# Moving tiles of one-pass float32 products: from starts on a multiple of 64 bytes to starts 8, 16, 24 and 48 bytes past one

## The chip, the core and the metric

The kernel runs on one core of a Trainium2 chip. The metric is the time of one execution on the device in microseconds (us), the median of several runs. A profile of one execution gives the details. Its engines are PE (TensorE, matrix products), PEld (TensorE's weight loads), DVE (VectorE), ACT (ScalarE), POOL (GpSimd) and SP (SyncE, here a queue of transfers).

A matrix product on TensorE has a stationary operand (`lhsT`, 128 x 128, loaded first as weights) and a moving operand (`rhs`, 128 partitions by up to 512 columns) that is read column by column from the on-chip memory SBUF. The change is about where in a partition of SBUF the moving operands begin.

## The reference, cut to what matters

```
attention, for each batch b and head h (8 x 8, 576 tokens, 64 per head):
    q_s = softmax of q over the 64 elements of a token
    k_s = softmax of k over the 576 tokens
    x   = q_s @ (k_s.T @ v)
x becomes 4608 tokens x 512
gated layer (512 -> 1536 -> 512):
    out = (sigmoid(x @ w_gate) * (x @ w_val)) @ w_out
```

All inputs are float32; the weights of the layer arrive as 64-bit words and are narrowed to float32 on the chip.

## The kernel before

**Tiling.** The 4608 tokens are done in 9 passes `w` of 512. A pass holds x transposed (512 features on 4 x 128 partitions, 512 tokens in the row) and runs over the 1536 hidden features in 6 steps of 256. Pass 0 is special: its products are plain float32 (`g1_0`, L610, and `g2_0`, L637), while the weights arrive and are narrowed and split beside it.

**Passes 1 to 8.** For these each float32 number is split into a high part of type float32r and the rest, low; a product takes three products of parts (high x high, high x low, low x high). Products of float32r pass the array once. The first layer (`g1`, L655) saves products by a scheme of Strassen's kind: the 2 x 2 blocks of x give seven combinations (B11, T1, T2, B21, T3, B22, T4), those of the weights seven (A11, S1, S2, A12, S3, S4, A22). A step of `g1` is 7 x 2 x 2 x 3 = 84 products with 256 columns. Stationary are the weights: `a_w` for A11, A12 and A22, `s_sb` for the sums S1 to S4. Moving are the split combinations of x, `c_hl`. They lie in four buffers with the tags c0 (B11, T1), c1 (T2, B21), c2 (T3, B22) and c3 (T4). The second layer (`g2`, L723) is 24 products with 512 columns a step: stationary the gated hidden values `h`, moving the split output weights `wo_hl`, two tiles a step, the first from the tag wo_hl, the second from the tag wo_t.

**What else lies in these buffers.** In pass 0 the c buffers hold raw weights on arrival (`w_raw` in c0 and c1, `wo_raw` in c3) and x of the pass (`x_0` in c2); wo_t and wo_hl hold the output weights while they are narrowed and split. The sums S1 to S4 and the split output weights go out to DRAM once and come back in each step: `s_load` (L278) for the next step after each product that used the sum, and `wo_load` (L234), both on POOL's queue.

**Order.** The order on each engine is written out by hand: in a step come the 84 products of `g1` with their evacuations (L673 to L696 on ACT and DVE), `h_split` (L705, L706), then a piece of the next pass's attention (`side_a`), `g2` of the step before, `wo_load`, and another piece (`side_b`). An engine does its instructions in this order and stops at the first that has to wait. The attention of the next pass runs through a chain of transfers on SP's queue: k_in and qn_in arrive (L331, L432), the rows' largest values go out and come back spread (`qn_send`, `q_spread`), qT_in arrives (L485) and is lessened by them on DVE (`qT_sub`, L489).

**Places in SBUF.** Tiles of a pool stand one behind the other, in order of the pools. The pads `pad_a` (48 floats, 192 bytes) and `pad_w` (80 floats, 320 bytes) shift what follows. Before the change, all c buffers, all wo_t and wo_hl buffers and the `ring` buffers begin 448 bytes past a multiple of 512; `s_sb`, `a_w` and `h` begin 128 bytes past one. All of these are multiples of 64 bytes, and the slices that the products read begin at multiples of 256 bytes within them.

Of the kernel before, what the change touches and what calls it, by code (L numbers as in the profile page):

```python
# [8 lines left out]
F32 = mybir.dt.float32  # L9
F32R = mybir.dt.float32r  # L10
I32 = mybir.dt.int32
# [6 lines left out]
P = 128  # L18
B, H, S, D = 8, 8, 576, 64
DM, DF = 512, 1536  # L20
NTOK = B * S
T = 512
HT = T // 2
NW = NTOK // T
NT = T // P
NP = H // 2
# [25 lines left out]
def attn_moe(ctx: ExitStack, tc: tile.TileContext, qf, qn, qT, k, kT, v, wg, wv, wo, out):  # L52
# [5 lines left out]
    cpool = ctx.enter_context(tc.tile_pool(name="cpool", bufs=1))  # L58
    apad = ctx.enter_context(tc.tile_pool(name="apad", bufs=1))
    apool = ctx.enter_context(tc.tile_pool(name="apool", bufs=1))  # L60
    two = ctx.enter_context(tc.tile_pool(name="two", bufs=2))
    wpad = ctx.enter_context(tc.tile_pool(name="wpad", bufs=1))
    wpool = ctx.enter_context(tc.tile_pool(name="wpool", bufs=2))
    four = ctx.enter_context(tc.tile_pool(name="four", bufs=4))
    ring = ctx.enter_context(tc.tile_pool(name="ring", bufs=11))
    small = ctx.enter_context(tc.tile_pool(name="small", bufs=2))
    apad.tile([P, 48], F32, name="pad_a")
    wpad.tile([P, 80], F32, name="pad_w")
    dpool = ctx.enter_context(tc.tile_pool(name="dpool", bufs=2, space=bass.MemoryType.DRAM))
    spool = ctx.enter_context(tc.tile_pool(name="spool", bufs=1, space=bass.MemoryType.DRAM))  # L70
    ps_acc = ctx.enter_context(tc.tile_pool(name="ps_acc", bufs=NT, space=bass.MemoryType.PSUM))
    ps_gv = ctx.enter_context(tc.tile_pool(name="ps_gv", bufs=3, space=bass.MemoryType.PSUM))
    ps_at = ctx.enter_context(tc.tile_pool(name="ps_at", bufs=1, space=bass.MemoryType.PSUM))

    s_sb = const.tile([P, 4, 2, 2, 2 * P], F32R, name="s_sb")
    x_32 = const.tile([P, NP, T], F32, name="x_32")
# [30 lines left out]
    w_raw = {}  # L107
    wo_raw = {}
    f_w = {}
    a_w = {}  # L110
    wo_t = {}

    def raw_tile(j):

        i = (0, 1, 2, 3, 0, 1, 2, 3, 0, 1, 2, 0)[j]
        if i == 2:
            return sg.rearrange("p q n t -> p (q n t)").bitcast(I32)
        if i == 3:
            return x_32.rearrange("p h t -> p (h t)").bitcast(I32)
        return cpool.tile([P, 4 * DM], I32, name="w_raw", tag=f"c{i}")  # L120

    def load_w(j):
        w_raw[j] = t = raw_tile(j).rearrange("p (n e) -> p n e", n=2)
        for n, src in enumerate((wg, wv)):
            nc.sync.dma_start(out=t[:, n], in_=src[j].bitcast(I32))

    def load_wo(j):
        if j % 3 == 0:
            wo_raw[j] = t = cpool.tile([P, 2 * DM], I32, name="wo_raw", tag="c3")
        else:  # L130
            wo_raw[j] = t = two.tile([P, 2 * DM], I32, name="wo_raw", tag="h_hi")
        nc.sync.dma_start(out=t, in_=wo[j * P:(j + 1) * P].bitcast(I32))
# [11 lines left out]
    def narrow_sign(raw):  # L144

        half = raw.bitcast(F16).rearrange("p (e f) -> p e f", f=4)
        nc.scalar.activation(
            half[:, :, 1], words(raw)[:, :, 1].bitcast(F32), AF.Copy, scale=2.0 ** -100
        )
# [8 lines left out]
    def narrow_abs(raw, w):  # L158
        src = words(raw)[:, :, 1].bitcast(F32)
        if len(w.shape) == 3:  # L160
            src = src.rearrange("p (a b) -> p a b", a=w.shape[1])
        nc.scalar.activation(w, src, AF.Abs, scale=2.0 ** -112)
# [33 lines left out]
    def wo_on_vector(j):  # L196
        return j % 2 and j > 6
# [5 lines left out]

    def wo_top(j):
        if j % 2 == 0:
            wo_t[j // 2] = wpool.tile([P, 2, DM], F32, name="wo_t")
        if not wo_on_vector(j):
            narrow_sign(wo_raw[j])
        narrow_abs(wo_raw[j], wo_t[j // 2][:, j % 2])
# [4 lines left out]
    wo_out = {}  # L214

    def wo_hi(j):
        wo_out[j] = t = wpool.tile([P, 2, DM], F32R, name="wo_hl")
        nc.scalar.copy(out=t[:, 0], in_=wo_t[j // 2][:, j % 2])

    def wo_save(j):  # L220
# [6 lines left out]
    wo_hl = {}  # L227

    def wo_load(w, p):
        wo_hl[w, p] = [  # L230
            wpool.tile([P, 2, DM], F32R, name="wo_hl", tag=tag) for tag in ("wo_hl", "wo_t")
        ]
        for i, t in enumerate(wo_hl[w, p]):
            nc.gpsimd.dma_start(  # L234
                out=t.rearrange("p h e -> p (h e)"), in_=wo_dram[2 * p + i].bitcast(F32R)
            )
# [308 lines left out]
        copy(out=x_32[:, hp], in_=x_ps.pop((w, hp)))  # L545


    x_0 = cpool.tile([P, NP, T], F32, name="x_0", tag="c2")
    q_0 = [two.tile([P, 2, T], F32, name="q_0", tag="h_lo") for _ in range(2)]

    def qT_copy(hp):
# [18 lines left out]
    def quarter(kh, th):  # L570
        return x_32[:, 2 * kh:2 * kh + 2, th * HT:(th + 1) * HT]

    c_32 = {}
    c_hl = {}
# [11 lines left out]

    def c_split(i):
        if i % 2 == 0:
            t = cpool.tile([P, 2 if i < 6 else 1, 2, 2, HT], F32R, name="c_hl", tag=f"c{i // 2}")
            for x in range(i, min(i + 2, 7)):  # L590
                c_hl[x] = t[:, x % 2]
        src = c_32.pop(i) if i in c_32 else quarter(*{B11: (0, 0), B21: (1, 0), B22: (1, 1)}[i])
        hi, lo = (c_hl[i][:, x] for x in range(2))
        nc.scalar.copy(out=hi, in_=src)
        nc.vector.tensor_tensor(out=lo, in0=src, in1=hi.bitcast(F32), op=ALU.subtract)
# [115 lines left out]
    def step(w, i):  # L711
        return (i - 1) % NS if w == 1 else i
# [114 lines left out]
    def after_first(j):  # L827
# [34 lines left out]
        if j == 10:  # L862
            c_subs()
            load_next(1, 5, range(2))
            for i in (B11, T1, T2, B21):
                c_split(i)
# [33 lines left out]
    for t in range(5):  # L900
        v_load(0, t, v0[:, t])
    load_wo(0)
    load_w(1)
    load_wo(1)
    load_w(2)
    for g in range(2):
        rows = kT[1, 2 * g * P:2 * (g + 1) * P].rearrange("(g p) s -> p g s", p=P)
        nc.sync.dma_start(out=k1T[:, 2 * g:2 * g + 2], in_=rows)
        for hp in (2 * g, 2 * g + 1):
            kT_load(1, hp, k1T[:, hp])  # L910
    load_w(3)
    load_wo(2)
    for c in range(NC):
        qn_load(1, c)
# [16 lines left out]
    for t in range(2, 5):  # L931
        n = KTILES[t][1]
# [65 lines left out]
    w_top(1)  # L998
    wo_low(0)
    wo_top(0)  # L1000
    w_low(2)
    wo_low(1)
# [3 lines left out]
    for j in range(NJ):  # L1006
# [5 lines left out]
        if j > 0:  # L1012
            wo_hi(j - 1)
        if j + 2 < NJ:
            w_top(j + 2)
        if j + 1 < NJ:
            w_join(j + 1)
            wo_top(j + 1)
# [24 lines left out]
        after_first(j)  # L1043

    wo_hi(NJ - 1)
    g_mul_0(NJ - 1)
    for i in (T3, B22, T4):
        c_split(i)
    wo_save(NJ - 1)

    def wo_next(w, at):
        wo_load(w, step(w, at))

    prev = None
    for w in range(1, NW):
        last = w == NW - 1
        for at in range(NS):
            p = step(w, at)
            end = last and at == NS - 1
            g1(w, p, None if end else step(w + (at + 1) // NS, (at + 1) % NS))  # L1060
            if at == NS - 1 and not last:
                for i in range(7):
                    c_split(i)
            h_split(w, p)
            if not last:
                side_a(w + 1, at)
            if prev is None:
                g2_0(NJ - 1)
                wo_next(1, 0)
                wo_next(1, 1)  # L1070
            else:
                g2(*prev)
                if not end:
                    wo_next(w + (at + 1) // NS, (at + 1) % NS)
            prev = (w, at)
            if not last:
                side_b(w + 1, at)
# [39 lines left out]
```

## Time and profile before

| | us |
|---|---|
| Median of three runs (980.42, 981.57, 981.74) | 981.57 |
| Span of the profiled execution (no other time of it is listed) | 984.2 |
| TensorE busy in it | 954.0 |
| VectorE busy | 613.1 |
| ScalarE busy | 471.4 |
| L655 (`g1`), busy, 4032 products | 483.1 |
| L723 (`g2`), busy, 1152 products | 272.3 |

The span runs from the first to the last instruction of the profiled execution. Rows of groups read: line, engine, operation, output<-input, shape, xcount | busy us, mean ns of one | idle us just before. Rows of stages read: stretch, its length, busy time and count for each engine, then the share of TensorE's clock that was granted, the busy share of the DMA engines, and GB/s. Rows of the timeline read: start, length, engine, line, operation, xcount, and in brackets the idle time before with what ended it. Products overlap: the next starts while the last columns of the one before drain, so the distance of two starts is shorter than the duration of one.

### The profile page before, as it was taken

The page shows a single profiled execution, that of the slowest core. Times are in us where ns is not written, and L with a number is a line of the kernel's source. Part 1 is how long each engine was busy: PE and PEld are TensorE (multiplying, and loading weights), DVE is VectorE, ACT ScalarE, POOL GpSimd, SP SyncE. Part 2 cuts the span into 40 slices and gives each one's busy share as a digit, 9 for nine tenths or more (in the row PEclk, how much of TensorE's full clock was granted, in tenths as well). Part 3 has the DMA queues.
Part 4 walks back from the last instruction along what each step waited for, and adds up shares of the span by engine and source line. Part 5 has one row for each costly group of instructions (what it writes and reads, how often), then busy time and mean ns, then how long its engine had stood idle before and what let it go on. Part 6 is the DMA issues. An engine that isn't in the chain of part 4 may idle for free.

```text
span 984.2 us, 15634 instructions
## 1 busy us (share of the span) xinstructions
PE 954.0 (97%) x6062; PEld 824.0 (84%) x6062; DVE 613.1 (62%) x1013; ACT 471.4 (48%) x812; POOL 167.3 (17%) x316
## 2 busy tenths in 40 slices
PE   5899999799999999999999999999999999999998
PEld 5544544599999999999989999899999999999997
DVE  8688778776666566755684667557654655463242
ACT  4589785553436354525362545353434434533222
POOL 0110001221122112111111111121112121212210
PEclk7899999899999999999999999999999999999999
DMA  9987484899699978998899869996998779858662
GB/s 337 330 244 267 165 291 166 302 350 323 203 245 361 306 229 212 374 284 259 180 381 304 261 143 375 332 276 132 374 317 239 216 237 312 248 176 251 199 206 74
DMA packets 93864, 257.78 MB, mean 262 GB/s; under 512 B 15264, under 2 KB 17568, under 8 KB 93024
## 3 DMA queue, kind: packets, MB, share of 16 engines
q0 software_dynamic: 43712, 168.32, 56.9%
q1 hardware_dynamic: 50080, 88.48, 30.6%
q8 instruction: 48, 0.79, 0.4%
q14 instruction: 24, 0.20, 0.1%
HBM read 228.20 MB, written 28.56 MB: 261 GB/s over the span
## 4 chain that ended last, share of the span: by engine, by line
PE 66%; DMA 17%; DVE 7%; ACT 7%; issue 2%; SPq 1%; POOL 0%; DVEq 0%; ACTq 0%; POOLq 0%
PE gv L655 37%; PE acc L723 19%; DMA ring<-k_in 3%; DMA q_m_row<-q_m 3%; PE gv L610 3%; DMA q_b<-q_m_row 3%; DMA kmax_row<-k_max 2%; PE gv L538 2%; DMA ring<-qT_in 1%; PE at L378 1%; PE acc L637 1%; DMA ring<-qn_in 1%; DMA s<-s_sb 1%; DMA wo<-wo_hl 1%; PE at L538 1%
## 5 line engine op out<-in xcount | busy, mean ns | idle before, releaser
L655 PE MATMUL gv<-c_hl,s_sb 128*128 128x256 f32 x2304 | 288.1, 280 | 4.3 <-ACT sg L673 4.2
L655 PEld LDWEIGHTS gv<-c_hl,s_sb 128*128 128x128 f32 x2304 | 276.7, 188 | 6.9 <-ACT sg L673 6.5
L723 PE MATMUL acc<-wo_hl,h 128*128 128x512 f32 x1152 | 272.2, 392 | 0.0
L723 PEld LDWEIGHTS acc<-wo_hl,h 128*128 128x128 f32 x1152 | 213.1, 188 | 44.3
L655 PE MATMUL gv<-c_hl,a_w 128*128 128x256 f32 x1728 | 226.1, 279 | 0.7 <-DVE a_w L269 0.7
L655 PEld LDWEIGHTS gv<-c_hl,a_w 128*128 128x128 f32 x1728 | 214.9, 188 | 5.2 <-issue 1.0
L278 POOL DMA_DIRECT2D s_sb<-s x188 | 100.1, 532 | 321.8 <-PE gv L655 317.5
L681 DVE TENSOR_TENSOR sg<-gv,sg 128x512 f32<-128x512 f32 x48 | 33.2, 691 | 163.0 <-PE gv L655 163.0
L234 POOL DMA_DIRECT2D wo_hl<-wo x96 | 50.9, 531 | 297.6 <-PE acc L723 295.4
L683 ACT COPY sg<-gv 128x512 f32<-128x512 f32 x48 | 28.1, 586 | 106.4 <-PE gv L655 106.4
L610 PE MATMUL gv<-x,f_w 128*128 128x512 f32 x160 | 72.4, 606 | 5.5 <-ACT h L618 5.5
L673 ACT COPY sg<-gv 128x512 f32<-128x512 f32 x48 | 28.0, 583 | 89.8 <-PE gv L655 65.1
L685 DVE TENSOR_TENSOR sg<-sg 128x512 f32<-128x512 f32 x48 | 33.2, 692 | 58.9 <-ACT sg L683 58.9
L610 PEld LDWEIGHTS gv<-x,f_w 128*128 128x128 f32 x160 | 30.5, 194 | 43.7 <-issue 36.0
L706 DVE TENSOR_TENSOR h<-sg,h 128x1024 fp32r<-128x1024 f32 x48 | 58.8, 1226 | 1.6
L688 ACT ACTIVATE sg<-sg 128x512 f32<-128x512 f32 x48 | 30.3, 632 | 55.8 <-DVE sg L687 55.8
L694 DVE TENSOR_TENSOR sg<-sg 128x512 f32<-128x512 f32 x48 | 33.2, 693 | 33.5 <-ACT sg L688 33.5
L637 PE MATMUL acc<-wo_t,h 128*128 128x512 f32 x96 | 45.3, 617 | 5.7 <-DVE h L622 5.6
L678 ACT COPY sg<-gv 128x512 f32<-128x512 f32 x48 | 28.1, 586 | 44.7 <-PE gv L655 44.7
L637 PEld LDWEIGHTS acc<-wo_t,h 128*128 128x128 f32 x96 | 18.8, 199 | 30.0 <-issue 21.7
L675 ACT COPY sg<-gv 128x512 f32<-128x512 f32 x48 | 28.1, 586 | 26.2 <-PE gv L655 26.1
L412 ACT CAST kv_sb<-kmax_b 64x256 fp32r<-64x256 f32 x14 | 5.7, 404 | 67.1 <-DVE kmax_b L388 66.8
(152 smaller groups left out, 1054.8 us busy)
## 6 DMA issues: line engine op xcount, KB each, us to landing
s_sb<-s POOLq DMA_DIRECT2D x188, 512.0 KB, 7.6
wo_hl<-wo POOLq DMA_DIRECT2D x96, 512.0 KB, 6.0
s<-s_sb POOLq DMA_DIRECT2D x6, 2048.0 KB, 7.6
out<-x SPq DMA_DIRECT2D x36, 256.0 KB, 9.6
ring<-k_in SPq DMA_DIRECT2D x28, 256.0 KB, 15.0
ring<-qn_in SPq DMA_DIRECT2D x28, 256.0 KB, 10.3
q_b<-q_m_row SPq DMA_DIRECT2D x56, 128.0 KB, 8.6
ring<-qT_in SPq DMA_DIRECT2D x28, 256.0 KB, 8.9
```

Of the source, the lines that this page charges most:

```text
L234: nc.gpsimd.dma_start(out=t.rearrange("p h e -> p (h e)"), in_=wo_dram[2 * p + i].bitcast(F32R))
L278: nc.gpsimd.dma_start(out=s_sb[:, i].rearrange("p h n e -> p (h n e)"), in_=s_dram[p][:, i * n:(i + 1) * n].bitcast(F32R),)
L538: nc.tensor.matmul(ps[:, f:t], lhsT=kl if lh else kh, rhs=rh[:, f:t], start=(lh == 0 and rh is qh), stop=(lh == 1),)
L610: nc.tensor.matmul(ps[n], lhsT=w[:, kt // 2, sl], rhs=x_0[:, kt], start=(kt == 0), stop=(kt == NK - 1),)
L637: nc.tensor.matmul(acc[0][m], lhsT=h_0[j][:, m * P:(m + 1) * P], rhs=wo_t[j // 2][:, j % 2], start=(j == 0), stop=(j == NJ - 1),)
L655: nc.tensor.matmul(ps[:, n], lhsT=lh(kt), rhs=c_hl[i][:, x, kt], start=(first and n == 0 and kt == 0 and lh is wh and x == 0), stop=(last ...
L681: nc.vector.tensor_tensor(out=sg[:, 0], in0=rr, in1=sg[:, 0], op=ALU.add)
L685: nc.vector.tensor_tensor(out=sg[:, 3], in0=sg[:, 3], in1=sg[:, 2], op=ALU.add)
L688: nc.scalar.activation(sg[:, 0:2, 0], sg[:, 0:2, 0], AF.Sigmoid)
L694: tt(out=sg[:, 0:2, 0], in0=sg[:, 0:2, 0], in1=sg[:, 0:2, 1], op=ALU.mult)
L706: nc.vector.tensor_tensor(out=lo, in0=sg[:, :, 0], in1=hi.bitcast(F32), op=ALU.subtract)
L723: nc.tensor.matmul(acc[w][m], lhsT=h[lh][:, i, sl], rhs=o[i][:, rh], start=(at == 0 and i == 0 and lh == 0 and rh == 0), stop=(at == NS - ...
```

## The change

The tiles that serve as moving operands get 16 floats more, and what is used of them starts 4, 12, 2, 6, 4 or 12 floats (16, 48, 8, 24, 16 or 48 bytes) behind the start of the buffer, by tag. The pads change with it, so that `a_w`, `h`, `four`, `ring` and all behind them stay where they were modulo 512 bytes. The c buffers, each 64 bytes longer, no longer stand at the same place modulo 512: with the shift, c2 begins 456, c0 16, c3 88 and c1 176 bytes past a multiple of 512. The wo_t buffers come to stand 240 and 304, the wo_hl buffers 336 and 400 past one (worked out from the order and the sizes of the pools). No instruction is added, removed or moved, and no number computed changes.

```
-    apad.tile([P, 48], F32, name="pad_a")
-    wpad.tile([P, 80], F32, name="pad_w")
+    apad.tile([P, 112], F32, name="pad_a")
+    wpad.tile([P, 16], F32, name="pad_w")
...
+    SHIFT = {"c0": 4, "c1": 12, "c2": 2, "c3": 6, "wo_hl": 4, "wo_t": 12}
+
+    def shifted(pool, n, dtype, name, tag):
+        k = SHIFT[tag]
+        return pool.tile([P, n + 16], dtype, name=name, tag=tag)[:, k:k + n]
...
-        return cpool.tile([P, 4 * DM], I32, name="w_raw", tag=f"c{i}")
+        return shifted(cpool, 4 * DM, I32, "w_raw", f"c{i}")
...
-            wo_raw[j] = t = cpool.tile([P, 2 * DM], I32, name="wo_raw", tag="c3")
+            wo_raw[j] = t = shifted(cpool, 2 * DM, I32, "wo_raw", "c3")
...
-            wo_t[j // 2] = wpool.tile([P, 2, DM], F32, name="wo_t")
+            wo_t[j // 2] = shifted(wpool, 2 * DM, F32, "wo_t", "wo_t").rearrange(
+                "p (h e) -> p h e", h=2
+            )
...
-        wo_out[j] = t = wpool.tile([P, 2, DM], F32R, name="wo_hl")
+        wo_out[j] = t = shifted(wpool, 2 * DM, F32R, "wo_hl", "wo_hl").rearrange(
+            "p (h e) -> p h e", h=2
+        )
...
-            wpool.tile([P, 2, DM], F32R, name="wo_hl", tag=tag) for tag in ("wo_hl", "wo_t")
+            shifted(wpool, 2 * DM, F32R, "wo_hl", tag).rearrange("p (h e) -> p h e", h=2)
+            for tag in ("wo_hl", "wo_t")
...
-    x_0 = cpool.tile([P, NP, T], F32, name="x_0", tag="c2")
+    x_0 = shifted(cpool, NP * T, F32, "x_0", "c2").rearrange("p (h t) -> p h t", h=NP)
...
-            t = cpool.tile([P, 2 if i < 6 else 1, 2, 2, HT], F32R, name="c_hl", tag=f"c{i // 2}")
+            n = 2 if i < 6 else 1
+            t = shifted(cpool, n * 4 * HT, F32R, "c_hl", f"c{i // 2}").rearrange(
+                "p (n h k t) -> p n h k t", n=n, h=2, k=2
+            )
```

## The prediction, made before the change was run

> **What bounds the kernel now.** I read the page's busy shares first, then the shares of the chain that ended last, then the busy time by stage, first of all instructions and then of the two lines whose moving tiles change.
>
> ```profile
> PE 954.0 (97%) x6062; PEld 824.0 (84%) x6062; DVE 613.1 (62%) x1013; ACT 471.4 (48%) x812; POOL 167.3 (17%) x316
> ...
> PE 66%; DMA 17%; DVE 7%; ACT 7%; issue 2%; SPq 1%; POOL 0%; DVEq 0%; ACTq 0%; POOLq 0%
> PE gv L655 37%; PE acc L723 19%; DMA ring<-k_in 3%; DMA q_m_row<-q_m 3%; PE gv L610 3%; DMA q_b<-q_m_row 3%; DMA kmax_row<-k_max 2%; PE gv L538 2%; DMA ring<-qT_in 1%; PE at L378 1%; PE acc L637 1%; DMA ring<-qn_in 1%; DMA s<-s_sb 1%; DMA wo<-wo_hl 1%; PE at L538 1%
> ```
>
> ```profile
> 182.00:484.00 302.00, 299.71 (x2130) 279.01 (x2129) 197.04 (x329) 140.66 (x262) 60.26 (x113) 1.00 0.98 277
> 484.00:787.00 303.00, 300.24 (x2130) 280.11 (x2129) 186.95 (x309) 137.06 (x254) 56.82 (x108) 1.00 0.97 280
> 787.00:984.00 197.00, 193.54 (x1334) 179.67 (x1332) 89.43 (x138) 66.11 (x121) 35.51 (x67) 1.00 0.72 213
> ```
>
> ```profile
> 181.60:984.00 802.40, 483.07 (x4032) 478.01 (x4032) 1.00 0.91 262
> ```
>
> ```profile
> 181.60:984.00 802.40, 272.25 (x1152) 213.10 (x1152) 1.00 0.91 262
> ```
>
> From 182 us on TensorE is busy all but 9 of 802 us (302 + 303 + 197 less 299.7 + 300.2 + 193.5), at the full granted clock (1.00 in the third column from the right). The last two rows are L655 alone (4032 products with 256 columns, moving tiles c_hl) and L723 alone (1152 products with 512 columns, moving tiles wo_hl): 483 and 272 us. Each of these products reads a tile that the change moves, so the start-to-start time of a product, which I call its pitch, decides. The timeline of TensorE gives it, since each row shows the start of a run of products and their count.
>
> ```profile
> 350.06 2.88 PE L655 MATMUL gv<-c_hl,s_sb 128*128 128x256 f32 x24
> 352.78 1.52 PE L655 MATMUL gv<-c_hl,a_w 128*128 128x256 f32 x12
> 354.14 2.88 PE L655 MATMUL gv<-c_hl,s_sb 128*128 128x256 f32 x24
> ...
> 358.22 5.66 PE L723 MATMUL acc<-wo_hl,h 128*128 128x512 f32 x24
> 363.72 2.50 PE L538 MATMUL gv<-ring,kv_sb 128*128 128x192 f32 x18
> ```
>
> ```profile
> 945.49 2.99 PE L655 MATMUL gv<-c_hl,s_sb 128*128 128x256 f32 x24
> 948.32 1.58 PE L655 MATMUL gv<-c_hl,a_w 128*128 128x256 f32 x12
> 949.73 2.99 PE L655 MATMUL gv<-c_hl,s_sb 128*128 128x256 f32 x24
> ...
> 953.97 5.67 PE L723 MATMUL acc<-wo_hl,h 128*128 128x512 f32 x24
> 959.48 1.58 PE L655 MATMUL gv<-c_hl,a_w 128*128 128x256 f32 x12
> ```
>
> The same instructions on the same tiles run in **two rhythms**. At 350 us 24 products take 2.72 us (352.78 - 350.06), 113.3 ns each; at 945 us they take 2.83 us, 117.9 ns each. A pass of 24 at L723 takes 5.50 us at 358 us and 5.51 us at 954 us: 229 ns each in both. Within a stretch the pitch is steady. The chain of waits, in order of time, shows whole stretches of 84 products (columns: start, us, what):
>
> ```profile
> 348.87 9.52 PE gv L655 x84
> ...
> 504.80 10.81 DMA q_m_row<-q_m
> 518.04 8.57 DMA q_b<-q_m_row
> 526.68 7.91 DMA ring<-qT_in
> ...
> 944.24 9.89 PE gv L655 x84
> 959.64 9.89 PE gv L655 x84
> ```
>
> Among the pieces that this view lists, 26 are whole stretches of 84; 5 of them take 9.52 us and 21 take 9.89 to 10.10. So four in five have the long pitch. As the rhythm changes between stretches and holds within them, it looks like a matter of how the reading falls against the lines of the memory, which a start address can touch.
>
> What would a product cost with no such loss? Products in plain float32 give a bound, because they read the same tiles and pass the array twice:
>
> ```profile
> 83.85 3.60 PE L637 MATMUL acc<-wo_t,h 128*128 128x512 f32 x8
> 87.28 3.17 PE L610 MATMUL gv<-x,f_w 128*128 128x512 f32 x7
> ```
>
> ```profile
> 625.38 1.95 PE L378 MATMUL at<-v,ring 128*128 128x128 f32 x16
> 627.16 3.04 PE L378 MATMUL at<-f_last,ring 128*128 128x128 f32 x24
> ```
>
> Eight of 512 columns take 3.43 us, 429 ns each, or 214 ns for each of two passes (that there are two is inferred from the time): 15 ns less than the 229 of L723. Sixteen of 128 columns, 256 column passes, take 1.78 us, 111 ns each, and each has a weight load, as each of L655 has. I take 111 ns and 214 ns as the floors of L655 and L723.
>
> The Trainium skill ("TensorE: Matmul & The Clock Gate", Back-to-back issue gap) gives N/2.4 + 2.5 ns for a single warm product, 109 and 216 ns here; the rows above stand 4 to 9 and 13 ns over it. If that held after the change, the sum below would come out at the second rival.
>
> **The change part by part.**
>
> *L655.* Nothing is added or removed: the same 4032 products, from tiles that start 8, 16, 24 or 48 bytes past a line. No row of before has a one-pass product that starts off a multiple of 64 bytes. The nearest is L365, whose moving tile has rows of 129 floats, so its starts walk 4 bytes at a time:
>
> ```profile
> L365 PE MATMUL acc<-lent x13: 269/274/422, 30.1 to 31.8; 128*128 128x129 f32 x9, 64*128 64x129 f32 x4
> ```
>
> ```profile
> L378 PE MATMUL at<-v,ring 128*128 128x128 f32 x112 | 13.6, 275 | 0.0
> ```
>
> Their median of 274 ns is the mean of the aligned L378 products, 275. So at half the reading rate a shifted start costs nothing; at the full rate it is open. Ends: all products at the floor, or one more 64-byte line for each product. A line is 16 columns, 117.9 / 16 = 7.4 ns. I take the value between, **the short pitch in all stretches**, since 113.3 ns is the pitch that the same products already reach and the rhythm depends on where the reading starts. By count 48 x 21/26 = 39 stretches gain 0.37 us (9.89 - 9.52): 14.3 us of TensorE time.
>
> *L723.* The pitch is 229 ns beside either pitch of L655, so I take no change; the ends are -15 ns (the floor) and +7.4 ns (a line) on 1152 products, -17 to +8.5 us.
>
> *What of a gain stays.* Not all of the loop is bound by TensorE. In the chain above the transfers of the attention side follow each other from 504.80 to 534.59 us (526.68 + 7.91), and VectorE waits for the last:
>
> ```profile
> 532.62 2.69 DVE L489 TENSOR_TENSOR ring<-ring,q_b 128x512 f32<-128x512 f32 x4 [4.94 <-DMA ring<-qT_in]
> ```
>
> A faster TensorE reaches that point sooner and waits there, because the products' evacuations stand behind L489 in VectorE's order. L655 has 37% of the 984.2 us on the chain, 364 of its 483 us: 0.75 of a gain stays. For L723 it is 19%, 187 of 272: 0.69. What is late next is the transfer of qT_in.
>
> So the sum is -14.3 x 0.75 = -10.7 us, and 0 from L723.
>
> *Transfers into shifted tiles.* 96 loads of wo_hl, and those of w_raw and wo_raw in the first loop, now land off a line.
>
> ```profile
> wo_hl<-wo POOLq DMA_DIRECT2D x96, 512.0 KB, 6.0
> ...
> w_raw<-wg_in SPq DMA_DIRECT2D x7, 512.0 KB, 5.8
> ...
> L723 PE MATMUL acc<-wo_hl,h 128*128 128x512 f32 x1152 | 272.2, 392 | 0.0
> ```
>
> ```profile
> 0.00:40.00 40.00, 29.68 (x125) 23.15 (x126) 28.40 (x48) 15.27 (x20) 3.85 (x10) 0.79 1.00 353
> ```
>
> L723 never waited (0.0 idle before it), and wo_hl lands after 6.0 us in a step of 15.4 (959.64 - 944.24): 9 us of cover, so nothing unless a load takes twice as long. The w_raw loads of the first 40 us stand on the path to the first products: 2 MB (two steps of two loads) at 353 GB/s are 6 us. A tenth more or less would be 0.6 us; I take 0.
>
> *VectorE and ScalarE on shifted tiles.* c_split writes 56 + 56 times into them.
>
> ```profile
> L595 DVE TENSOR_TENSOR c_hl<-ring,c_hl 128x512 fp32r<-128x512 f32 x32 | 21.2, 684 | 0.0
> ```
>
> One more step in 16 would be 43 ns each, 112 x 43 ns = 4.8 us in all, on engines busy 62% and 48%. TensorE's work covers it except at the start of each of 8 passes, where one or two splits are on the path: 0.7 us at most, either way. I take 0. The pads keep all other tiles at the same place modulo 512 bytes, so nothing else moves.
>
> **The sum.** The profiled execution has a span of 984.2 us, 2.6 us above the median of the three runs, 981.6; no other time of it is listed. Differences go onto the median: 981.6 - 10.7 = **970.9 us**.
>
> **The rivals.**
>
> 1. *The loss goes altogether.* All products at the floor: 14.3 us, plus (113.3 - 111) x 4032 = 9.3 us, times 0.75, and 17 x 0.69 for L723: 17.7 + 11.7 = 29.4, so 952 us. For it: the loss is only in one-pass products. Against: no row shows one without it.
> 2. *Nothing depends on the start.* L365 speaks for it. The rhythms fall as before: 981.6 us. That would also be the time if what matters is only the moment at which a stretch starts.
> 3. *One more line for each product* (slower). A tile of 1024 bytes that starts 8 bytes past a line covers 17 lines, not 16. If the reading of lines is what limits the one-pass products, as the loss at full rate suggests, each pays 7.4 ns: 4032 + 1152 of them, 38 us, less some 8 us of waits (3 of 302, 3 of 303 and more by the stage rows) that the longer pitch fills: 1012 us. It decides as soon as the lines and not the columns set the pitch; with half of the price, 996 us.
> 4. *The long pitch everywhere* (slower). The remaining fifth of the stretches, 9 of 48, lose 0.37 us: +3.4 us, 985 us. For it: 21 of 26 already sit there.
> 5. *A finer line* (slower). If lines of 4 columns count, only starts at 8 and 24 bytes cross one more: the products T3, B22 and T4, 3 of 7, 1728 in all, 4 x 117.9 / 256 = 1.8 ns each: +3.2 us, 985 us. The Trainium skill ("SBUF — State Buffer", Door 1: The DMA port swizzle) says lines are 16 bytes and that an access that crosses to a new one pays; no run here shows it yet, and L365, which crosses such lines at each of its starts, shows no price.
>
> **How the numbers follow.** Forecast 0.32, loss gone 0.20, no dependence 0.15, one more line 0.17, long pitch 0.11, finer line 0.05. I lean to faster because four in five stretches are in the worse of two rhythms and the floor lies further off, so that a shift of the reading has more to gain than to lose; the bound on the other side is as large, so the lean is weak. Faster by over 0.2% (2 us, about what a measurement of this kernel can tell from no change) 0.52, within 0.15, slower 0.33. The range takes in the floor (952, less 2) and the half-price line (996) with room to 1006; beyond lie most of rival 3's full price and a little of the open ends. The forecast's own range is 964 to 977.
>
> **What would show it.** Right: the chain's stretches of 84 take 9.52 us throughout, L723's passes of 24 still 5.50 us, and the waits at L489's transfer grow by about 0.5 us a pass. Loss gone: stretches of 9.3 us and passes near 5.15. Wrong: stretches over 9.9 us in all steps (rival 3: about 10.5, with L723 near 5.7), or a pitch that differs between products of one stretch by the tile's offset, which none of the stretches shows now; stretches of 9.52 and 9.89 in the old mixture would be rival 2. A wait of L723 for wo_hl would show that the transfers suffer.

## The result and the profile after

The changed kernel takes 992.7 us (median of four runs, 991.6 to 994.9), the kernel before 981.7 in the same comparison: slower by 1.2%, ratio 1.0121 with a 95% interval of 1.0105 to 1.0138. The forecast was 970.9 us. The time lies inside the stated range, on the other side of no change: 11.0 us slower where 10.7 us faster was forecast. That is luck: the upper part of the range was put there for another loss, one more line in every product, which did not come.

The page of the changed kernel, busy time by engine and the chain that ended last:

```profile
PE 963.7 (97%) x6062; PEld 830.1 (84%) x6062; DVE 612.3 (62%) x1013; ACT 472.1 (48%) x812; POOL 166.8 (17%) x316
...
PE 76%; ACT 7%; issue 5%; DMA 5%; DVE 5%; SPq 1%; POOL 0%; POOLq 0%; DVEq 0%; ACTq 0%
```

TensorE is busy 9.7 us longer with the same 6062 products, and VectorE, ScalarE and GpSimd are as before. TensorE's share of the chain rose from 66% to 76%, and that of the transfers fell from 17% to 5%. The two lines of products, now L669 (L655 before) and L737 (L723 before), in the view by stage, each alone; the first row leaves out the first and last few products:

```profile
181.60:989.00 807.40, 488.94 (x4013) 484.97 (x4012) 1.00 0.90 260
```

```profile
178.00:989.00 811.00, 276.13 (x1152) 213.07 (x1152) 1.00 0.89 260
```

L737 went from 272.25 to 276.13 us at the same count and the same granted clock. The timeline of TensorE, one whole step near the end, shows where L669 lost; the five rows of a step are the products B11, then T1 and T2, B21, T3 and B22, and T4:

```profile
853.41 1.58 PE L669 MATMUL gv<-c_hl,a_w 128*128 128x256 f32 x12
854.83 3.01 PE L669 MATMUL gv<-c_hl,s_sb 128*128 128x256 f32 x24
857.68 1.58 PE L669 MATMUL gv<-c_hl,a_w 128*128 128x256 f32 x12
859.10 3.02 PE L669 MATMUL gv<-c_hl,s_sb 128*128 128x256 f32 x24
861.96 1.61 PE L669 MATMUL gv<-c_hl,a_w 128*128 128x256 f32 x12
863.41 5.74 PE L737 MATMUL acc<-wo_hl,h 128*128 128x512 f32 x24
868.99 2.22 PE L549 MATMUL gv<-ring,kv_sb 128*128 128x512 f32 x9
```

The difference of two starts over the count gives the pitch: 118.3, 118.8, 118.3, 119.2 and 120.8 ns, then 232.5 at L737. Before, 41 of the 48 steps in the trace had one pitch throughout, 10 of them 113.3 ns and 31 of them 117.8; in the other 7 the pitch changed at the pause between T1 and T2. Now it depends on the buffer, and no stretch has the short one. The chain of waits confirms it for whole steps:

```profile
837.95 10.03 PE gv L669 x84
853.57 10.00 PE gv L669 x84
```

A step of 84 takes 10.0 us where it took 9.52 or 9.89.

For finer comparison I use the mean time between two starts that follow each other, over all products of a kind in the one trace that each kernel has, with times over 130 ns (L655) and 260 ns (L723) left out as pauses. Before, that is 116.6 and 229.1 ns. After, 119.3 and 232.5: by buffer 118.6 in c0 (shift 16), 118.3 in c1 (48), 120.1 in c2 (8), 121.3 in c3 (24), and 231.1 to 234.3 in the four buffers of the output weights. With unrounded means that is (119.3 - 116.6) x 4032 = 10.8 us and (232.5 - 229.1) x 1152 = 4.0 us: 14.8 us more at the pitch, where the medians of the runs differ by 11.0.

### The profile page after: what moved, and what is told of

It is laid out like the page before. It is cut to its first block, busy times and chain, and to the rows that moved or that the text cites. A ratio compares the mean times of both kernels' runs of the same rounds, so it can differ in the third digit from the quotient of the medians.

```text
span 990.4 us, 15634 instructions
## 1 busy us (share of the span) xinstructions
PE 963.7 (97%) x6062; PEld 830.1 (84%) x6062; DVE 612.3 (62%) x1013; ACT 472.1 (48%) x812; POOL 166.8 (17%) x316
## 4 chain that ended last, share of the span: by engine, by line
PE 76%; ACT 7%; issue 5%; DMA 5%; DVE 5%; SPq 1%; POOL 0%; POOLq 0%; DVEq 0%; ACTq 0%
PE gv L669 46%; PE acc L737 24%; PE at L389 3%; PE gv L549 2%; ACT ring L368 2%; ACT ring L468 1%; DMA wo_raw<-wo_in 1%; DMA x<-wv_in 1%; DMA w_raw<-wg_in 1%; PE acc L651 1%; ACT kt L324 1%; DMA ring<-k_in 1%; DMA s<-s_sb 1%; ACT L468 1%; PE at L549 1%
## 5 line engine op out<-in xcount | busy, mean ns | idle before, releaser
L669 PE MATMUL gv<-c_hl,s_sb 128*128 128x256 f32 x2304 | 292.5, 282 | 1.5 <-ACT sg L687 1.5
L669 PEld LDWEIGHTS gv<-c_hl,s_sb 128*128 128x128 f32 x2304 | 282.0, 189 | 3.1 <-ACT sg L687 3.1
L737 PE MATMUL acc<-wo_hl,h 128*128 128x512 f32 x1152 | 276.1, 395 | 0.0
L737 PEld LDWEIGHTS acc<-wo_hl,h 128*128 128x128 f32 x1152 | 213.1, 188 | 48.1
L669 PE MATMUL gv<-c_hl,a_w 128*128 128x256 f32 x1728 | 230.6, 282 | 0.0
L669 PEld LDWEIGHTS gv<-c_hl,a_w 128*128 128x128 f32 x1728 | 219.1, 188 | 4.5 <-issue 0.7
L695 DVE TENSOR_TENSOR sg<-gv,sg 128x512 f32<-128x512 f32 x48 | 33.2, 691 | 178.7 <-PE gv L669 178.7
L701 DVE TENSOR_TENSOR sg<-gv,sg 128x512 f32<-128x512 f32 x48 | 33.2, 692 | 6.3
```

The costliest lines, as they stand in the source:

```text
L669: nc.tensor.matmul(ps[:, n], lhsT=lh(kt), rhs=c_hl[i][:, x, kt], start=(first and n == 0 and kt == 0 and lh is wh and x == 0), stop=(last ...
L695: nc.vector.tensor_tensor(out=sg[:, 0], in0=rr, in1=sg[:, 0], op=ALU.add)
L701: nc.vector.tensor_tensor(out=sg[:, 1], in0=z, in1=sg[:, 1], op=ALU.add)
L737: nc.tensor.matmul(acc[w][m], lhsT=h[lh][:, i, sl], rhs=o[i][:, rh], start=(at == 0 and i == 0 and lh == 0 and rh == 0), stop=(at == NS - ...
```

## The experiments

**Two theories.** A: the start of the moving tile inside a line sets the pitch, as the change intends. B: what counts is where the buffers came to stand. The change makes them 64 bytes longer, so that they no longer stand at one place modulo 512 bytes, against weights that all stand at 128. In what follows, *distance* is the start of the moving tile minus that of the stationary one, in bytes and modulo 512. It was 320 in every product of L655 and L723 before.

Short diffs follow; where only the table of shifts differs, it is given against the changed kernel, and where only pads differ, against the kernel before.

### Shifts taken out, longer buffers kept

```
-    SHIFT = {"c0": 4, "c1": 12, "c2": 2, "c3": 6, "wo_hl": 4, "wo_t": 12}
+    SHIFT = {"c0": 0, "c1": 0, "c2": 0, "c3": 0, "wo_hl": 0, "wo_t": 0}
```

> The longer buffers and the new pads stay, but all six shifts are 0, so every moving tile starts on a multiple of 64 bytes again; only its place modulo 512 bytes is that of the changed kernel (c0 0, c1 128, c2 448, c3 64). Theory A (the start inside a line sets the pitch): the two rhythms of before come back, L655 at 113.3 or 117.8 ns, L723 at 229, and about 981 to 983 us. Theory B (the place modulo 512, against the weights at 128, sets it): the pitch stays at 118 to 121 ns by tile, L723 at 232 to 233, and about 992 us.

Measured: 989.7 us against 981.6, ratio 1.0088 (1.0068 to 1.0108). The timeline of a step:

```profile
821.55 1.60 PE L669 MATMUL gv<-c_hl,a_w 128*128 128x256 f32 x12
822.99 3.04 PE L669 MATMUL gv<-c_hl,s_sb 128*128 128x256 f32 x24
825.87 1.60 PE L669 MATMUL gv<-c_hl,a_w 128*128 128x256 f32 x12
827.30 2.99 PE L669 MATMUL gv<-c_hl,s_sb 128*128 128x256 f32 x24
830.13 1.57 PE L669 MATMUL gv<-c_hl,a_w 128*128 128x256 f32 x12
831.54 5.67 PE L737 MATMUL acc<-wo_hl,h 128*128 128x512 f32 x24
837.06 1.12 PE L669 MATMUL gv<-c_hl,a_w 128*128 128x256 f32 x8
```

All tiles start on a multiple of 64 bytes, and yet B11 has 120.0 ns (1.44 us for 12), T1 and T2 120.0, B21 119.2, T3 and B22 117.9, T4 117.5. (Starts are shown to 0.01 us, so 12 products give a pitch to some 0.8 ns; the means over all steps are 119.25 ns in c0, 119.67 in c1, 117.95 in c2 and 117.42 in c3.) The cheap ones are c2 and c3, which stand at 448 and 64; the dear ones c0 and c1, at 0 and 128. Theory A falls as the main cause: 8.0 of the 11.0 us are there without any shift (by the intervals, 8 and 11 are each known to about 2 us). L737 splits too, by its four buffers: 229.8 ns at distance 64, 233.0 at 128, 233.3 at 192, 227.2 at 256.

### Shifts of 8 and 24 replaced by 16 and 48

```
+    SHIFT = {"c0": 4, "c1": 12, "c2": 4, "c3": 12, "wo_hl": 4, "wo_t": 12}
```

> c2 and c3 are shifted by 16 and 48 bytes instead of 8 and 24, all else as in the changed kernel. Theory A1 (lines of 16 bytes count: a start off a multiple of 16 costs 2 to 3 ns beyond the rest): T3, B22 and T4 fall from 120.0, 120.4 and 121.3 ns to 118.4, as in c0 and c1, which is 1152 x 1.8 + 576 x 2.9 = 3.7 us of TensorE time, so about 989 us. Rival A2 (any start off a multiple of 64 costs, by an amount that hangs on the buffer): they stay at 120 to 121 and 992 us. Theory B also says that they stay.

Measured: 992.0 us, ratio 1.0114 (1.0093 to 1.0135), and the runs scatter from 988.3 to 993.8. In the total no gain can be told. In the pitches there is one: T3 and B22 fall from 120.1 to 119.3 ns, T4 from 121.3 to 117.4, while c0 and c1 stay to 0.05 ns. So a start off a multiple of 16 looks dearer, but the shift also changes the distance (c3 from 472 to 496), and c2 stays above 118.4. This run alone can't tell the two apart.

### Shifts dealt out anew

```
+    SHIFT = {"c0": 2, "c1": 6, "c2": 4, "c3": 8, "wo_hl": 2, "wo_t": 8}
```

> The shifts are dealt out anew: c0 8, c1 24, c2 16, c3 32, wo_hl 8, wo_t 32 bytes. Theory A1: the costly pitch goes with the shift, so B11, T1 (8) and T2, B21 (24) rise to 120 to 121 ns, T3, B22 (16) fall to 118.4, T4 (32) is 117.8 to 118.5; at L723 the products of wo_hl (8) rise above 234, those of wo_t (32) stay at 229 to 233. Theory B and rival A2: the pitch goes with the buffer, as in the changed kernel. Time in A1: 4 of 7 products at the dearer pitch, about 993 us.

Measured: 996.6 us in one run. c0 rose from 118.6 to 120.6 ns with its shift of 8, c1 from 118.3 to 120.3 with 24, c3 fell from 121.3 to 118.7 with 32; c2 with 16 bytes has 119.6. The dear pitch goes with the shifts that are no multiple of 16, as A1 (lines of 16 bytes) said, by some 2 to 3 ns, though c2 does not come down to the 118.4 of A1 and every distance changed along with the shift. But L723's four buffers have 232.7 to 233.5, and the 32-byte ones hardly less (232.9 against 233.5), where A1 put those at 229 to 233 and the others over 234.

### All moving tiles 32 bytes on

```
+    cpad.tile([P, 8], F32, name="pad_c")
-    apad.tile([P, 48], F32, name="pad_a")
-    wpad.tile([P, 80], F32, name="pad_w")
+    apad.tile([P, 40], F32, name="pad_a")
+    wpad.tile([P, 88], F32, name="pad_w")
+    fpad.tile([P, 120], F32, name="pad_f")
```

The pools cpad and fpad are new and hold only these pads, ahead of cpool and of `four`.

> The sizes of before, with pads that put all c, wo_t and wo_hl buffers 480 bytes past a multiple of 512 instead of 448, so 32 past a multiple of 64, the same for all; the rest stays where it was modulo 512. Theory A with lines of 64 bytes: no stretch at 113.3 ns, all at 117.8 to 118.5, L723 at 231 to 233, about 988 us. Theory A1 with lines of 16 bytes alone, or a line of 32: as before, both rhythms and 982 us. Theory B: a new place against the weights, so another pitch than 113 or 118, either way.

Measured: 996.7 us, ratio 1.0153 (1.0136 to 1.0169): the slowest. L655 runs at 120.0 ns in all products, L723 at 233.4. One step of 32 bytes for all, distance 352 instead of 320, costs more than the whole change. That fits B, and neither form of A, which gave at most 118.5 ns for L655.

### The same distance made in two ways

The first kernel moves the weights on (with them the other tiles of the pools `const`, `apool` and `two`), the second the moving tiles back, both to a distance of 256.

```
+    const.tile([P, 16], F32, name="pad_s")      first kernel only
+    cpad.tile([P, 112], F32, name="pad_c")
-    apad.tile([P, 48], F32, name="pad_a")
-    wpad.tile([P, 80], F32, name="pad_w")
+    apad.tile([P, 64], F32, name="pad_a")
+    wpad.tile([P, 64], F32, name="pad_w")
+    fpad.tile([P, 16], F32, name="pad_f")       second kernel only
```

> The kernel before, with its moving tiles where they were (448 past a multiple of 512), but s_sb, a_w and h moved from 128 to 192: moving minus stationary is 256 instead of 320. If the distance of moving and stationary tiles sets the pitch, L723 runs at 227 ns (the wo_hl buffer of the first experiment at distance 256: 227.2) instead of 229, and L655 leaves the pair 113.3 and 117.8. If the place of the moving tile alone sets it, nothing changes: 229 ns, both rhythms and 982 us.

> The kernel before, with s_sb, a_w and h where they were (128), but the c, wo_t and wo_hl buffers moved from 448 to 384: the distance is again 256. If the distance sets the pitch, this kernel has the pitches of the one with the weights moved, in both lines, and L723 is at 227 ns. If the place of the moving tile sets it, L723 is at 227 ns here (the buffer at 384 had it) but not there.

Measured, against 982.4: 992.4 us with the weights moved, ratio 1.0100 (1.0079 to 1.0120), and 991.9 with the moving tiles moved, 1.0100 (1.0082 to 1.0117). Timeline of the first, then of the second:

```profile
824.68 3.04 PE L658 MATMUL gv<-c_hl,s_sb 128*128 128x256 f32 x24
827.56 1.60 PE L658 MATMUL gv<-c_hl,a_w 128*128 128x256 f32 x12
829.00 3.04 PE L658 MATMUL gv<-c_hl,s_sb 128*128 128x256 f32 x24
831.88 1.60 PE L658 MATMUL gv<-c_hl,a_w 128*128 128x256 f32 x12
833.32 5.63 PE L726 MATMUL acc<-wo_hl,h 128*128 128x512 f32 x24
838.79 1.48 PE L658 MATMUL gv<-c_hl,a_w 128*128 128x256 f32 x11
```

```profile
823.90 3.04 PE L659 MATMUL gv<-c_hl,s_sb 128*128 128x256 f32 x24
826.78 1.60 PE L659 MATMUL gv<-c_hl,a_w 128*128 128x256 f32 x12
828.22 3.04 PE L659 MATMUL gv<-c_hl,s_sb 128*128 128x256 f32 x24
831.10 1.60 PE L659 MATMUL gv<-c_hl,a_w 128*128 128x256 f32 x12
832.54 5.63 PE L727 MATMUL acc<-wo_hl,h 128*128 128x512 f32 x24
838.00 1.60 PE L659 MATMUL gv<-c_hl,a_w 128*128 128x256 f32 x12
```

Row for row the same: 24 products in 2.88 us (120.0 ns), 24 of the second layer in 5.47 and 5.46 us (228 ns). In the first kernel the moving tiles stand where they stood before modulo 512, and the loss is there. So **it is the distance of the moving tile from the stationary one that sets the pitch**, not the place of either.

### The places not yet seen

The longer buffers with no shift, moved on by other pads.

```
-    SHIFT = {"c0": 4, "c1": 12, "c2": 2, "c3": 6, "wo_hl": 4, "wo_t": 12}
-    apad.tile([P, 112], F32, name="pad_a")
-    wpad.tile([P, 16], F32, name="pad_w")
+    SHIFT = {"c0": 0, "c1": 0, "c2": 0, "c3": 0, "wo_hl": 0, "wo_t": 0}
+    cpad.tile([P, 64], F32, name="pad_c")
+    apad.tile([P, 48], F32, name="pad_a")
+    wpad.tile([P, 80], F32, name="pad_w")
```

> No shifts; the longer buffers stand at the places that have not been seen: c2 192, c0 256, c3 320, c1 384 (distances 64, 128, 192, 256), wo_t 448 and 0, wo_hl 64 and 128 (distances 320, 384, 448, 0). If the distance modulo 256 is enough, L655 has for T3, B22 at 64 what it had at 320 (117.8, or 113.3), for B11, T1 at 128 what it had at 384 (119.2), for T4 at 192 what it had at 448 (117.4), for T2, B21 at 256 what it had at 0 (119.3 to 120.0); L723 has at 320 229.8 as at 64, at 384 233.0 as at 128, at 448 233.3 as at 192, at 0 227.2 as at 256. If it is modulo 512 or the absolute place, these pairs differ.

Measured: 990.3 us in one run. The pairs agree to 0.02 ns: c2 at distance 64 has 117.95 ns, and had 117.95 at 320; c3 at 192 has 117.42, as at 448; c1 at 256 119.34 with s_sb and 120.00 with a_w, 119.33 and 120.00 at 0. L723: 229.83, 232.95, 233.33 and 227.15 at 320, 384, 448 and 0, against 229.83, 232.96, 233.33 and 227.15 at 64, 128, 192 and 256. The distance counts modulo 256 bytes.

### Inside a line, all else at the old distance

c2, c0 and c1 get 256 bytes more and a shift of 8, 16 and 32 bytes inside, so that all other distances stay 64 modulo 256; the pads are those of before.

```
-    SHIFT = {"c0": 4, "c1": 12, "c2": 2, "c3": 6, "wo_hl": 4, "wo_t": 12}
+    SHIFT = {"c0": 4, "c1": 8, "c2": 2, "c3": 0, "wo_hl": 0, "wo_t": 0}
...
-        k = SHIFT[tag]
-        return pool.tile([P, n + 16], dtype, name=name, tag=tag)[:, k:k + n]
+        k, more = SHIFT[tag], 64 if tag in ('c2', 'c0', 'c1') else 0
+        return pool.tile([P, n + more], dtype, name=name, tag=tag)[:, k:k + n]
```

> The layout of before modulo 256 bytes (distance of moving and stationary 64 in all products), but c2 starts 8, c0 16 and c1 32 bytes further, each in a buffer that is 256 bytes longer: distances 72, 80 and 96; c3 and the output weights are left at 64. If the distance modulo 256 sets the pitch also inside a line, T3, B22 (72) are near the 120.1 ns that the changed kernel has at this distance, B11, T1 (80) at 119 to 119.5, T2, B21 (96) near 120.0, T4 and L723 (64) at 117.8 and 229 as before. If the start off a line of 16 bytes is what costs, T3 and B22 stand out and B11 to B21 stay near 117.8.

Measured: 988.6 us in one run. T3 and B22 (shift 8) 119.6 ns, B11 and T1 (16) 118.9, T2 and B21 (32) 119.3 and 120.0; T4 and L723, unmoved, 117.9 and 229.2 as before. All three shifts cost, and the 32-byte one, which starts on a multiple of 16, as much as the 8-byte one. So the distance acts in steps of less than 64 bytes as well, or a start off a multiple of 64 costs by itself. Whether the start off 16 adds something of its own is left to the next run.

### Moving and stationary tile both 8 bytes on

c2 and s_sb both get 256 bytes more and a shift of 8 bytes; the other tiles stand as before, modulo 256.

```
-    s_sb = const.tile([P, 4, 2, 2, 2 * P], F32R, name="s_sb")
+    s_all = const.tile([P, 4 * 4 * 2 * P + 64], F32R, name="s_sb")
+    s_sb = s_all[:, 2:2 + 4 * 4 * 2 * P].rearrange("p (s h n e) -> p s h n e", s=4, h=2, n=2)
...
+    SHIFT = {"c0": 0, "c1": 0, "c2": 2, "c3": 0, "wo_hl": 0, "wo_t": 0}
```

> c2 and s_sb both start 8 bytes further than in the kernel before. T3 and B22 then have the old distance of 64, with both tiles off a line of 16 bytes; T1 and T2 have the distance 56, with the moving tile on a line. If only the distance counts: T3 and B22 at 117.8 (or 113.3) as before, T1 and T2 at another pitch. If the moving tile's start off a line of 16 costs by itself: T3 and B22 at about 120, T1 and T2 at 117.8. B11, B21 and T4 (a_w, c0, c1, c3 unmoved) stay in any case but for the rhythm that they take over.

Measured: 991.6 us in one run. The timeline:

```profile
823.47 1.57 PE L670 MATMUL gv<-c_hl,a_w 128*128 128x256 f32 x12
824.88 2.97 PE L670 MATMUL gv<-c_hl,s_sb 128*128 128x256 f32 x24
827.69 1.58 PE L670 MATMUL gv<-c_hl,a_w 128*128 128x256 f32 x12
829.10 3.04 PE L670 MATMUL gv<-c_hl,s_sb 128*128 128x256 f32 x24
831.98 1.57 PE L670 MATMUL gv<-c_hl,a_w 128*128 128x256 f32 x12
```

T3 and B22 have the distance of before, 64, with both tiles off a line: 2.88 us for 24, 120.0 ns (119.9 in the mean). T1 and T2 have the same shifted weights, moving tiles on a line and the distance 56: 2.81 us, 117.1 (117.3 in the mean). So with both tiles 8 bytes off and the distance unchanged, a product costs some 2 ns more. That it is the moving tile is argued: in T1 and T2 the weights alone are off and nothing is lost, but their distance of 56 was seen nowhere else. Over all the kernels, the first layer's moving tiles off a multiple of 16 had 119.6 to 121.3 ns by buffer, those 16, 32 or 48 bytes past a multiple of 64 had 117.4 to 120.1; no run has one of the latter at the distance 64.

### Looking for a better place

Three kernels use the distances that looked best: L723 at 0 (227 ns) with L655 at 64; L655 at 192 with L723 at 0; L655 at 192 with L723 at 64. Only the pads of the kernel before change:

```
+    cpad.tile([P, 96], F32, name="pad_c")       second and third
-    apad.tile([P, 48], F32, name="pad_a")
+    apad.tile([P, 80], F32, name="pad_a")       second and third
-    wpad.tile([P, 80], F32, name="pad_w")
+    wpad.tile([P, 64], F32, name="pad_w")       first and second
+    fpad.tile([P, 16], F32, name="pad_f")       first and second
```

> The kernel before with wo_t and wo_hl moved from 448 to 384, so that L723 has the distance 0 modulo 256 and L655 keeps 64. By the distance: L723 at 227 to 228 ns instead of 229.1, 1152 x 1.2 = 1.4 us less on TensorE, of which 0.7 stays: 980.5 to 981 us if L655 keeps its mixture of 113.3 and 117.8. The rival: the rhythm in which L655 starts is handed on by L723, so its mixture changes, by up to 13 us less or 5 us more.

> The kernel before with the c buffers at 320 (distance 192 modulo 256 in all of L655) and wo_t and wo_hl at 384 (distance 0). T4 alone at 192 had 117.4 ns in two runs. If that pitch holds for all of L655, it loses 0.8 ns on 4032 products against the mean of 116.6 of before, +3.2 us, and L723 gives back 1.4: about 983 us. If 192 has a short rhythm as 64 has, it may be 113.3 in some stretches, and the time below 981.

> The kernel before with the c buffers at 320 (distance 192 modulo 256 in L655), wo_t and wo_hl left at 448 (distance 64 in L723). By the distances the pitches are 113.3 or 117.8 ns in L655 and 229 in L723, as in the kernel before; only the mixture of the two rhythms can differ, since L723 hands another rhythm on. All at 113.3: 13 us of TensorE time less, of which 0.7 stays, so 972 us; all at 117.8: 5 us more, 986. If the mixture is a matter of the waits and not of the place, it is that of before and the time is the same.

Measured: 986.3 us against 983.9, ratio 1.0025 (1.0005 to 1.0045); 983.4 against 983.9, 1.0005 (0.9985 to 1.0025); 981.5 against 983.5, 0.9990 (0.9971 to 1.0009). None beats the kernel before. The pitches came as the distances said: L723 at 228.1, 227.1 and 229.5 ns, L655 at 113.3 or 117.8 in all three. But the first had hardly a stretch at 113.3 (mean 117.5), which by the pitches costs 3.6 us of TensorE's time where L723 gave 1.2. The timeline of the third shows how the rhythm changes:

```profile
784.38 1.57 PE L657 MATMUL gv<-c_hl,a_w 128*128 128x256 f32 x12
785.79 3.13 PE L657 MATMUL gv<-c_hl,s_sb 128*128 128x256 f32 x24
788.76 1.52 PE L657 MATMUL gv<-c_hl,a_w 128*128 128x256 f32 x12
790.12 2.88 PE L657 MATMUL gv<-c_hl,s_sb 128*128 128x256 f32 x24
792.84 1.52 PE L657 MATMUL gv<-c_hl,a_w 128*128 128x256 f32 x12
```

B11 takes 1.41 us for 12 (117.5 ns). Where T1 ends and T2 begins there are two short pauses, in which starts are 188 and 220 ns apart, and from then on the pitch is 113.3 (1.36 us for 12). In the kernel before, pauses at the same place also lead from 113.3 to 117.8. What decides which of the two follows was not found.

## Why the prediction was wrong

**Where the argument held.** TensorE bounds the loop, and the pitch of the two lines decided. The transfers and the splits cost nothing, as put: the loads of wo_hl land after 6.3 us instead of 6.0, L737 never waits for them, and the splits of c_hl (L609) take 684 ns as before. That a part of a change of TensorE's time vanishes in waits held too. The sizes, 0.75 and 0.69 by the chain, are not shown: 11.0 of 14.8 us is 0.74, but that sets medians of runs against two single traces. Between the traces the span grew by 6.2 us. Of the 14.8 us, 5.4 were taken back by fewer pauses inside L655 (39 over 130 ns before, 23 after), and the products of other lines took 3.1 less. The profiled execution of before was also longer than the median one: a time was 1.7 to 1.8 us above its span wherever both are listed, which makes about 986.0 us of its 984.2, against 981.7. So the agreement with 0.75 may be chance.

**The step that failed** is "I take the value between, **the short pitch in all stretches**" for L655, and with it "I take no change" for L723. Both came from reading the two rhythms as a matter of how the moving tile falls against its own lines. The rows of before spoke against it: the same products on the same tiles run in both rhythms, so the start of a tile can't be what chooses between them, and inside a step the rhythm changed only at a pause. The change kept every other tile in place modulo 512, as the prediction noted, "so nothing else moves"; but the longer buffers moved against the weights, from one distance, 64 modulo 256, to eight between 16 and 216. The list of places ahead of the prediction holds all of these, and they were not in the sum. Shown by the runs: instead of the 3.3 ns that the short pitch would have gained, L655 lost 2.7, and L723 lost 3.4 where none was put; with no shift at all the moved buffers cost 8.0 us (L655 +2.1 ns, L723 +1.7); and moving the weights alone, with the moving tiles of both lines where they were modulo 512, cost 10.0 us (L655 +3.3 ns, L723 -1.2). One of the signs of being wrong that were named ahead is what the timeline shows, a pitch that differs inside a stretch by the tile, but the offset that decides is the one against the weights.

**The rivals.** *Loss gone* is out: no distance that was tried gives L655 less than 113.3 or L723 less than 226.6 ns in any long stretch. *No dependence* is out, since the pitch follows the place. *One more line*, 7.4 ns a product, is out: the dearest buffer pays 3.5 ns over 117.8, and no run shows the line of 64 bytes from which that price was worked out. *The long pitch everywhere* is part of what happened: no step of the changed kernel has 113.3, which by the pitches is (117.8 - 116.6) x 4032 = 4.7 of the 10.8 us of L655. *A finer line* was right in kind: T3, B22 and T4, with starts at 8 and 24, are the dearest in the changed kernel, and at a fixed distance a start 8 bytes off, of both tiles, costs 2.1 ns (119.9 against 117.8) where 1.8 was put. The Trainium skill ("SBUF — State Buffer", Door 1: The DMA port swizzle) says that lines are 16 bytes and that going to a new one costs. The run with both tiles 8 bytes on agrees with it, but does not tell 16 bytes from a longer line. Such starts explain the smaller part of the loss: the remaining 3 of the 11 us hold it and the shifts' own changes of distance together, and the run with 16 and 48 bytes could not tell them apart in the total.

**What stays open.** That the reading of the weights for the next product and the reading of the moving tile hinder each other when they stand at certain distances is what the distances suggest; no run shows the readings themselves. The Trainium skill ("TensorE: Matmul & The Clock Gate", Step-by-step: what each phase is for) says that TensorE has two independent read ports and that loading the next weights takes nothing from the running product. By that the place of the weights should not matter; in the kernel with the weights moved, moving them alone changed the pitch of L655 from 116.6 to 119.9 ns. Also open is what chooses between 113.3 and 117.8 ns after a pause, and how much of L737's 3.4 ns is due to its shifts of 16 and 48 bytes (the moved buffers alone made 1.7 of it).

## What to carry to other kernels

When a kernel is bound by one-pass float32 products, note for each line of products the starts of both tiles modulo 256 bytes, and compare them before and after an edit that only changes a tile's length: 64 bytes more in each buffer, with no shift, cost 0.9% here, with no instruction changed. A shift of all moving tiles doesn't test where they start, because it also shifts them against the weights; move the weights along, or move the weights alone, to tell the two apart. And keep the moving tile on a multiple of 64 bytes where you can: 8 bytes off, at an unchanged distance, cost 2.1 ns a product.

## What the runs showed of the hardware

- The pitch of one-pass products (229 ns with 512 columns, where plain float32 takes 429) depends on the distance of moving and stationary tile modulo 256 bytes. With 256 columns and both tiles on multiples of 64: 113.3 or 117.8 ns at 64 and 192, 119.2 at 128, 119.3 to 120.0 at 0. With 512 columns and all buffers at one distance: 228.0 at 0, 229.1 at 64; in mixed layouts: 227.2 at 0, 229.8 at 64, 233.0 at 128, 233.3 at 192. The distance 0, best for the one, is the worst of these for the other. These are means in a sequence: what the products before them do shifts them by up to some ns (L723 at 128 and at 192 was seen only beside buffers at other distances).
- At distances 64 and 192, the same products run in either of two steady rhythms, 113.3 and 117.8 ns, and change at pauses as short as 0.1 us.
- Plain float32 products are nearly free of all this: 429 ns with 512 columns before, and after the change 429 where the moving tile is wo_t and a median of 431 where it is x_0, which starts 8 bytes past a multiple of 64.
